# An explicit sequence of all operations in place of a list scheduler

## The chip, the cores and the metric

The kernel runs on one core of a Trainium2 chip. A core has five instruction queues that matter here: TensorE (PE, matrix products; its weight loads are listed as PEld), VectorE (DVE), ScalarE (ACT), GpSimd (POOL) and SyncE (SP, which issues nearly all DMAs). Each queue runs its instructions in the order in which the program holds them; an instruction waits for the semaphores of those it depends on, and what is behind it in the same queue waits with it. The metric is the device time of one execution in microseconds (us).

## The reference

One transformer block on x of 2048 rows by 640 columns, in fp32:

```python
h  = x + A(layernorm(x))                 # wqkv 640 x 1920, wo 640 x 640
h2 = h + B(layernorm(h))                 # w_gate, w_up 640 x 1728, w_down 1728 x 640
# A: 32 heads of 20; row s attends to rows s, s-2, ..., s-14 (rows < 0 masked)
logits = einsum("bhsd,bhswd->bhsw", q, kg) * 20 ** -0.5
o      = einsum("bhsw,bhswd->bhsd", softmax(logits), vg)      # then o @ wo
# B
g = silu(x @ w_gate); u = x @ w_up; return (g * u) @ w_down
```

## The kernel before

**Tiling.** The 2048 rows are worked on in four blocks of 512 rows, each of four tiles of 128. The 640 columns are five chunks of 128 for contraction, and four groups of 160 (eight heads) for attention. The FFN's 1728 columns are 14 slices of 128 (the last is half full). Each fp32 operand of a product is split into a high and a low part of the fp32r type, and each product takes three passes: high by high, low by high, high by low. ScalarE makes the high parts by a cast, VectorE the low ones by a subtraction.

**Stages of a block.** x is loaded and normalised; TensorE transposes it into a PSUM bank (L604), ScalarE and VectorE split it into high and low (L606, L607). The wqkv weights are loaded (L616) and split (L617, L619), and projected with (L643, 480 columns at a time); the results are evicted (L648) and stored to DRAM, from where attention loads q, k and v back in a layout with eight shifted rows. Attention is mostly VectorE's: a product of 128x2560 elements for q times k (L692), a reduction of it (L699), softmax (L706 to L723), the product with v (L727), and a tree of additions (L735). The output is transposed, multiplied by wo (L890), and added to x. Then the second normalisation (L507 writes its low parts into `shb`) and the FFN: for each slice the weights are loaded (L938) and split (casts L939 for gate and up, L940 for down, subtraction L956; low parts are kept in DRAM and loaded again in later blocks, L951 and L944). TensorE computes the gate into bank 5 (in the listings `bank_73`) and the up projection into bank 6 (`bank_74`), 15 matmuls each (L962). ScalarE applies silu to bank 5 (L985), VectorE multiplies by bank 6 (L986), the result is split (L996, L997) and the down products (L973) gather in banks 0 to 4. In the last two blocks some slices are done in pairs, with combined operands that need fewer products (L1046, L1068, L1093, L1103), and the remaining down products come at the very end (L1298), followed by the last additions (L1109).

Attention of one block and the FFN of another run side by side: the VectorE instructions of attention fill the time in which TensorE does the FFN.

**What sets the order.** No engine's program is written out by hand. Each operation (one or several instructions of one engine) is recorded by `P.add(engine, cost, function, reads, writes, priority, ...)`; there are 2846, and their dependencies follow from the addresses that they read and write. At the end `for n in P.order(): P.ops[n][2]()` emits them, so the sequence of `order()` is the order of each queue. Before, `order()` first simulates the five engines and the DMA lanes by the recorded costs and takes the ready operation with the best priority (`listed`), then goes nine times through a round (`ROUNDS`) in which due times are worked out backwards (`latest`) and the simulation is repeated with them. Each operation's place is its simulated start plus, for some 320 operations, a number of us from the table `SHIFT`; the result is the topological order by that key.

## Time and profile before

| | |
|---|---|
| timed runs | median 837.33 us of 3 (836.17 to 838.05) |
| profiled execution | span 835.3 us (it has no time of its own beside the span) |
| granted clock of TensorE | 0.999 |
| TensorE busy | 826.3 us (99%), 4061 matmuls |
| VectorE busy | 755.7 us (90%), 916 instructions |
| ScalarE busy | 421.3 us (50%), 740 instructions |
| GpSimd busy | 23.1 us (3%) |
| DMA | 211.08 MB, mean 253 GB/s |

The span goes from the first to the last instruction of the profiled execution. "Busy" is the time in which an engine had an instruction in work; the idle time between is put down to what ended it. In rows such as `L986 DVE TENSOR_TENSOR fa<-bank,fa ... x34 | 23.2, 682 | 4.1 <-ACT fa L985 2.1` one reads the line, the engine, the operation, its output and inputs, the count, the busy time in us and the mean of one in ns, and after the second bar the engine's idle time just before these instructions with what ended most of it. In a row of waits, `PE bank L604 <- DVE sha L607: 1.4, 1, 1.4`, the first part is the instruction that waited, the second what it waited for, then the total in us, the number of waits and the longest.

### The profile page before, as it was taken

The numbers are of one execution on the slowest core, as the hardware profiler recorded it, in microseconds if no ns is written. First come the engines' busy times: TensorE is split into PE (matmuls) and PEld (weight loads), VectorE is DVE, ScalarE is ACT, GpSimd is POOL, SyncE is SP. The second block draws the span as 40 slices with busy tenths as digits, with TensorE's granted clock in tenths as the row PEclk, the third lists the DMA queues.
The fourth block names the chain that finished last, engine by engine and source line by source line (L and its number), as shares of the span: only waits on it lengthen the run. The fifth ranks groups of instructions, "written<-read, shape, count | busy, mean of one in ns | idle before, by whom it ended". The sixth has DMA issues, their size and how long they took to land.

```text
span 835.3 us, 11299 instructions
## 1 busy us (share of the span) xinstructions
PE 826.3 (99%) x4061; PEld 712.8 (85%) x4061; DVE 755.7 (90%) x916; ACT 421.3 (50%) x740; POOL 23.1 (3%) x34
## 2 busy tenths in 40 slices
PE   8999999999999999999999999999999999999998
PEld 6888888889978888887888888888988888888998
DVE  7599999999999999999999999998869888777982
ACT  7856473333783435654543476565695323323440
POOL 0000000000100000001000000000000000000000
PEclk9999999999999999999999999999999999999999
DMA  8897868568679764899899758899999634457722
GB/s 274 288 348 275 267 213 283 185 207 308 186 219 343 257 197 177 326 303 349 282 313 349 271 173 315 255 288 352 352 339 320 224 115 151 124 175 258 273 99 75
DMA packets 113223, 211.08 MB, mean 253 GB/s; under 512 B 37952, under 2 KB 70400, under 8 KB 112528
## 3 DMA queue, kind: packets, MB, share of 16 engines
q1 hardware_dynamic: 112864, 209.96, 74.0%
q8 instruction: 32, 0.52, 0.2%
q10 hardware_dynamic: 304, 0.41, 0.1%
q14 instruction: 23, 0.19, 0.1%
HBM read 151.27 MB, written 59.05 MB: 252 GB/s over the span
## 4 chain that ended last, share of the span: by engine, by line
PE 84%; DVE 8%; ACT 3%; DMA 3%; issue 1%; SPq 0%; POOL 0%; DVEq 0%; ACTq 0%; POOLq 0%
PE bank L962 22%; PE bank L1046 18%; PE bank L643 15%; PE bank L973 10%; PE bank L1298 7%; PE bank L890 6%; DMA fa<-in_x_dram 2%; PE bank L1103 1%; DVE fa L692 1%; PE bank L1093 1%; DVE fa L735 1%; PE bank L1068 1%; DVE fa L727 1%; DVE fa L699 1%; ACT ra L617 1%
## 5 line engine op out<-in xcount | busy, mean ns | idle before, releaser
L962 PE MATMUL bank<-shb,ra 128*128 128x512 f32 x810 | 190.0, 390 | 1.3 <-DVE shb L507 1.3
L962 PEld LDWEIGHTS bank<-shb,ra 128*128 128x128 f32 x810 | 151.4, 188 | 32.7 <-ACT shb L506 1.5
L643 PE MATMUL bank<-ra,sha 128*128 128x480 f32 x480 | 105.2, 379 | 0.2 <-ACT ra L617 0.2
L643 PE MATMUL bank<-ra,shb 128*128 128x480 f32 x470 | 102.5, 378 | 0.0
L643 PEld LDWEIGHTS bank<-ra,sha 128*128 128x128 f32 x480 | 89.8, 188 | 14.5 <-ACT ra L617 0.6
L643 PEld LDWEIGHTS bank<-ra,shb 128*128 128x128 f32 x470 | 88.1, 188 | 13.2
L692 DVE TENSOR_TENSOR fa<-fa 128x2560 f32<-128x2560 f32 x32 | 90.2, 2820 | 0.9 <-DMA fa<-qsc 0.4
L727 DVE TENSOR_TENSOR fa<-fa 128x2560 f32<-128x2560 f32 x32 | 90.3, 2822 | 0.8
L699 DVE TENSOR_REDUCE fa<-fa 128x128 f32<-128x2560 f32 x32 | 89.9, 2810 | 0.4
L1046 PE MATMUL bank<-shb,ra 128*128 128x512 f32 x360 | 89.4, 395 | 0.6 <-DVE fa L990 0.6
L973 PE MATMUL bank<-ra,acts 128*128 128x512 f32 x328 | 80.7, 391 | 0.0
L1046 PEld LDWEIGHTS bank<-shb,ra 128*128 128x128 f32 x360 | 66.0, 188 | 16.2 <-DVE fa L1223 1.7
L735 DVE TENSOR_TENSOR fa<-fa 128x1280 f32<-128x1280 f32 (+2 forms) x70 | 76.7, 1096 | 1.3
L890 PE MATMUL bank<-ra 128*128 128x320 f32 x480 | 74.1, 310 | 0.0
L890 PEld LDWEIGHTS bank<-ra 128*128 128x128 f32 x480 | 71.7, 188 | 2.4 <-ACT fa L893 1.0
L648 ACT ACTIVATE st<-bank,fa 128x480 f32<-128x480 f32 x64 | 41.0, 656 | 64.1 <-PE bank L643 59.5
L973 PEld LDWEIGHTS bank<-ra,acts 128*128 128x128 f32 x328 | 61.1, 188 | 13.2 <-DVE acts L997 0.5
L1046 PE MATMUL bank<-ra 128*128 128x512 f32 x288 | 69.1, 390 | 0.0
L1046 PEld LDWEIGHTS bank<-ra 128*128 128x128 f32 x288 | 53.9, 188 | 11.1
L1223 DVE TENSOR_TENSOR fa<-bank,fa 128x512 f32<-128x512 f32 x60 | 41.0, 689 | 19.8 <-PE bank L1046 19.0
L939 ACT CAST ra<-fa 128x1280 fp32r<-128x1280 f32 (+1 forms) x38 | 45.6, 1207 | 22.9 <-PE bank L962 12.3
L996 ACT CAST acts<-fa 128x512 fp32r<-128x512 f32 x34 | 21.0, 620 | 48.7 <-DVE fa L986 47.0
(189 smaller groups left out, 1059.8 us busy)
## 6 DMA issues: line engine op xcount, KB each, us to landing
fa<-in_ffn_dram SPq DMA_DIRECT2D x28, 960.0 KB, 6.4
fa<-ksc SPq DMA_DIRECT2D x16, 880.0 KB, 5.4
fa<-vsc SPq DMA_DIRECT2D x16, 880.0 KB, 7.3
ra<-lsc SPq DMA_DIRECT2D x21, 640.0 KB, 5.8
ra<-lsc SPq DMA_DIRECT2D x27, 320.0 KB, 3.7
lsc<-ra SPq DMA_DIRECT2D x13, 640.0 KB, 4.6
fa<-in_ffn_dram SPq DMA_DIRECT2D x12, 640.0 KB, 4.0
ra<-tsc SPq DMA_DIRECT2D x8, 960.0 KB, 7.1
```

Source lines behind the costliest of these rows:

```text
L643: T.matmul(banks[bk][:, 0:480], l, r_(wq(g, w, c), 480), start=(p, c) == first_mm, stop=(p, c) == last_mm)
L648: P.add("ACT", act(480) + 0.06, lambda bk=bk, j=j: A.activation(stage_t()[:, so : so + 1920].rearrange("p (t j c) -> p t j c", t=3, j=NJ)[ ...
L692: P.add("DVE", dve(2560), lambda: V.tensor_tensor(f(PROD, 2560).rearrange("p (j w c) -> p j w c", j=2, w=W), window(ko, 2 * jp), f(qo + 32 ...
L699: P.add("DVE", dve(2560), lambda: V.tensor_reduce(f(lo + 128 * jp, 128), f(PROD, 2560).rearrange("p (n d) -> p n d", d=DH), axis=AX.X, op= ...
L727: V.tensor_tensor(f(PROD, 2560).rearrange("p (j w d) -> p j w d", j=2, d=DH), bass.AP(tensor=fa[:, vo : vo + 160].tensor, offset=fa[:, vo ...
L735: V.tensor_add(dst(v), v[:, :, 0:m, :], v[:, :, m : 2 * m, :])
L890: T.matmul(banks[bk][:, 0:320], l, r_(m, 320), start=p == 0 and c == 0, stop=p == 2 and c == NC - 1)
L939: P.add("ACT", act(n), lambda: A.copy(r_(gu, n), f(raw, n)), r=[rf(raw, n)], w=[rr(gu, n)], prio=PR["fh"])
L962: T.matmul(banks[bk], r_(gu + 1280 * w + wid * c + col, 128), x2(a, c), start=p == 0 and c == 0, stop=p == 2 and c == NC - 1)
L973: T.matmul(banks[bk][:, lo:hi], l, m, start=first and p == 0, stop=last and p == len(passes) - 1)
L1046: T.matmul(banks[bk], r_(ws[w] + 256 * q, 128), x(a, c), start=start and p == n == q == 0, stop=stop and p == 2 and n == len(terms) - 1 an ...
L1298: T.matmul(banks[bks[j]][:, 0:320], t(a, 128, 128 * j), r_(ws[w], 320), start=p == q == 0, stop=p == NP - 1 and q == 2)
```

## The change

The table `SHIFT`, the rounds, `listed` and `latest` are removed. `ORDER` is a tuple of all 2846 operation numbers; `order()` is now the topological order by the place in it. The operations, their numbers, their dependencies and their tiles are the same: 4061 matmuls, 916 VectorE instructions and 586 DMAs of SyncE in both programs; only ScalarE has 33 loads of an activation table where it had 32, as its functions come in another succession. Since the file has another length, a line of the part after the table has a number higher by 12 (L962 becomes L974, L985 becomes L997, L986 becomes L998), and three tiles have other numbers behind their names.

```diff
-LANES, HOP = 8, 0.035
-LAP = {"PE": 0.0, "ACT": 0.1, "DVE": 0.08, "POOL": 0.0, "SP": 0.0}
...
-SHIFT = {
-    7: 3.5, 9: -106.8, 22: 0.4, 31: -515.8, 32: -221.5, 33: -238.8, 34: -84.5, 35: -34.6, 36: -483.8, 37:
...
+ORDER = (
+    0, 6, 11, 42, 3, 10, 7, 9, 2, 31, 32, 34, 12, 13, 15, 8, 16, 17, 39, 33, 36, 37, 118, 43, 22, 14, 40, 119, 38,
...
     def order(self):
-        start = self.listed()
-        for stretch, serial, dma in ROUNDS:
-            start = self.listed(self.latest(start, stretch, dma), serial)
-        self.start, self.end = start, max(t + o[1] for t, o in zip(start, self.ops))
-        ops = self.ops
-        left = [len(o[3]) for o in ops]
-        key = [(t + SHIFT.get(n, 0.0), n) for n, t in enumerate(start)]
-        heap, out = [key[n] for n in range(len(ops)) if not left[n]], []
+        left = [len(o[3]) for o in self.ops]
+        succ = [[] for _ in self.ops]
+        for n, o in enumerate(self.ops):
+            for d in o[3]:
+                succ[d].append(n)
+        place = {n: i for i, n in enumerate(ORDER)}
+        heap, out = [(place.get(n, n), n) for n in range(len(left)) if not left[n]], []
         heapq.heapify(heap)
         while heap:
             n = heapq.heappop(heap)[1]
             out.append(n)
-            for m in self.succ[n]:
+            for m in succ[n]:
                 left[m] -= 1
                 if not left[m]:
-                    heapq.heappush(heap, key[m])
+                    heapq.heappush(heap, (place.get(m, m), m))
         return out
```

The moves are spread over the whole program: on TensorE 808 operations lie on average 4.0 places from where they were (at most 65), on ScalarE 579 by 3.3, on VectorE 855 by 4.3 (at most 92), on SyncE 586 by 6.1 (at most 103); GpSimd is unchanged. Three places follow, each as rows of one engine's queue: line, operation, output and inputs, size, and how many in a row.

**The start on TensorE**, before: matmuls that warm the array up (L554, `bank_72`), transposes of x (L604) and the first QKV projections (L643).

```order
L554 MATMUL bank_72<-ra 128x512 x10
L604 MATMUL bank_75<-fa 128x128
L604 MATMUL bank_74<-fa 128x128 x8
L554 MATMUL bank_72<-ra 128x512
L604 MATMUL bank_73<-fa 128x128 x3
L604 MATMUL bank_75<-fa 128x128 x4
L643 MATMUL bank_69<-ra,sha_128 128x480
L604 MATMUL bank_74<-fa 128x128 x4
```

and now:

```order
L566 MATMUL bank_72<-ra 128x512 x11
L616 MATMUL bank_74<-fa 128x128 x4
L616 MATMUL bank_75<-fa 128x128
L655 MATMUL bank_68<-ra,sha_124 128x480 x2
L655 MATMUL bank_68<-ra,sha_125 128x480
L655 MATMUL bank_68<-ra,sha_124 128x480 x2
L616 MATMUL bank_74<-fa 128x128 x4
```

Five transposes instead of sixteen stand ahead of the first projection, and further tiles' transposes come between projections. On SyncE the first loads were one of x with 64 rows, three tiles of x, then eight of wqkv; now they are that of 64 rows, one wqkv, one tile of x, six wqkv, two tiles of x. On ScalarE two casts of wqkv now stand ahead of the first cast of the transposed x.

**The gates near 450 us on TensorE**, around one slice's up projection into `bank_74`; `bank_73` is the gate's, and rows with `acts` are down products. Before:

```order
L962 MATMUL bank_74<-shb,ra 128x512 x15
L973 MATMUL bank_72<-acts,ra 128x512 x3
L973 MATMUL bank_68<-ra,acts 128x512 x3
L973 MATMUL bank_69<-ra,acts 128x512 x3
L973 MATMUL bank_70<-ra,acts 128x512 x3
L973 MATMUL bank_71<-ra,acts 128x512 x3
L962 MATMUL bank_73<-shb,ra 128x512 x15
L962 MATMUL bank_74<-shb,ra 128x512 x15
```

and now (the first row of `bank_74` ends the same slice's projection, the second begins the next slice's):

```order
L985 MATMUL bank_72<-acts,ra 128x512 x9
L985 MATMUL bank_68<-ra,acts 128x512 x3
L974 MATMUL bank_74<-shb,ra 128x512 x5
L985 MATMUL bank_69<-ra,acts 128x512 x6
L985 MATMUL bank_68<-ra,acts 128x512 x3
L974 MATMUL bank_74<-shb,ra 128x512 x5
L985 MATMUL bank_70<-ra,acts 128x512 x3
```

Projections come in pieces of five between down products, and the next slice's up projection begins ahead of its gate projection: `bank_74` is written again after nine matmuls, where thirty lay between before (three in each of five groups, and fifteen of the gate).

**VectorE near 500 us**, around the multiply that reads `bank_74` (L986, now L998), among instructions of attention. Before:

```order
L723 TENSOR_TENSOR fa<-fa 128x256
L896 TENSOR_TENSOR h_1559<-h_1559,fa 128x640
L727 TENSOR_TENSOR fa<-fa 128x2560
L735 TENSOR_TENSOR fa<-fa 128x2x640
L986 TENSOR_TENSOR fa<-bank_74,fa 128x512
L735 TENSOR_TENSOR fa<-fa 128x2x2x160
L727 TENSOR_TENSOR fa<-fa 128x2560
```

and now:

```order
L735 TENSOR_TENSOR fa<-fa 128x256
L739 TENSOR_TENSOR fa<-fa 128x2560
L747 TENSOR_TENSOR fa<-fa 128x2x640
L747 TENSOR_TENSOR fa<-fa 128x2x2x160
L739 TENSOR_TENSOR fa<-fa 128x2560
L747 TENSOR_TENSOR fa<-fa 128x2x640
L998 TENSOR_TENSOR fa<-bank_74,fa 128x512
```

Three attention instructions that stood behind the multiply now stand ahead of it.

93 lines of the change are left out of this document (1 added, 92 removed), and 175 rows, old and new, of tables (ORDER, SHIFT).

## The prediction

> **What bounds the kernel now.** I read the page's totals first, then the forty slices, then the shares of the chain of waits.
>
> ```profile
> PE 826.3 (99%) x4061; PEld 712.8 (85%) x4061; DVE 755.7 (90%) x916; ACT 421.3 (50%) x740; POOL 23.1 (3%) x34
> PE   8999999999999999999999999999999999999998
> PE 84%; DVE 8%; ACT 3%; DMA 3%; issue 1%; SPq 0%; POOL 0%; DVEq 0%; ACTq 0%; POOLq 0%
> ```
>
> TensorE is busy for 826.3 of 835.3 us, and only the first and the last slice show a gap; the chain that ended last runs through it for 84%. The reordering changes no operation, so the only thing to gain is idle time of TensorE, 9.0 us in all. The view by windows tells where that lies (from:to, the window's length, then busy time and count of PE, PEld, DVE, ACT and POOL, the granted clock, the DMA share and GB/s):
>
> ```profile
> 0.00:20.00 20.00, 16.99 (x73) 13.81 (x74) 15.96 (x46) 15.39 (x40) 1.16 (x7) 1.00 0.84 273
> 180.00:240.00 60.00, 58.62 (x315) 52.91 (x314) 59.36 (x58) 33.71 (x72) 3.90 (x4) 1.00 0.69 224
> 400.00:460.00 60.00, 60.00 (x266) 49.51 (x265) 59.45 (x57) 26.24 (x35) 1.72 (x2) 1.00 0.94 322
> 770.00:835.30 65.30, 61.45 (x419) 61.19 (x418) 46.64 (x83) 21.62 (x36) 0.00 (x0) 0.99 0.45 159
> ```
>
> 3.0 us are idle in the first 20 us, 1.4 between 180 and 240, and 3.85 in the last window. The last cannot move: the final matmuls end at 769.86 + 60.29 = 830.15 us (chain row below), and the last additions and the stores of the output follow. The waits of TensorE name the rest:
>
> ```profile
> PE bank L604 <- DVE sha L607: 1.4, 1, 1.4
> PE bank L554 <- POOL ra L1401: 1.3, 1, 1.3
> PE bank L962 <- DVE shb L507: 1.3, 1, 1.3
> PE bank L1046 <- DVE fa L990: 0.6, 1, 0.6
> PE bank L604 <- DVE fa L443: 0.2, 1, 0.2
> PE bank L643 <- ACT ra L617: 0.2, 1, 0.2
> ```
>
> The L554 row is the start of the program (nothing can be ahead of it). The five others add up to 3.7 us. **That is the most that an order can win among waits shown as idle**; a loss has no such limit, because VectorE is 59.45 of 60 us busy in the window 400 to 460 and has nothing to give back when TensorE is kept waiting for it.
>
> **The head.** From the timeline of the start:
>
> ```profile
> 1.31 4.64 PE L554 MATMUL bank<-ra 128*128 128x512 f32 x10 [1.31 <-POOL ra L1401]
> 3.31 4.69 SPq L616 DMA_DIRECT2D fa<-in_wqkv_dram  x8
> 8.41 0.66 PE L604 MATMUL bank<-fa 128*128 128x128 f32 x4 [1.40 <-DVE sha L607]
> 11.22 11.09 PE L643 MATMUL bank<-ra,sha 128*128 128x480 f32 x50
> ```
>
> Before, sixteen transposes L604 stand ahead of the first QKV projection L643, and at 8.41 four of them wait 1.40 us for L607 to empty their bank; the projections run without a break from 11.22. In the new order five transposes stand ahead of it, so that wait can go (at most −1.4). Against it, SyncE now puts one wqkv load ahead of all but the first x load and six more ahead of the last two, and ScalarE has two wqkv casts ahead of its cast of the transposed x. A wqkv cast takes 0.599 us (the L617 row below), so if both were in the way the projections would start 1.2 us later. I take −0.4, between −1.4 and +1.2 and on the side of the gain, since eleven transposes fewer stand ahead of the projections, but the row at 3.31 puts 4.69 us on the issuing of the eight loads, which the casts now need sooner. A second spot is the last wqkv load:
>
> ```profile
> 50.15 0.59 ACT L617 CAST ra<-fa 128x480 fp32r<-128x480 f32 x1 [1.17 <-DMA fa<-in_wqkv_dram]
> 50.79 3.54 PE L643 MATMUL bank<-ra,sha 128*128 128x480 f32 x14 [0.16 <-ACT ra L617]
> L617 ACT CAST ra<-fa 128x480 fp32r<-128x480 f32 x20 | 10.9, 599 | 1.2 <-DMA fa<-in_wqkv_dram 1.2
> ```
>
> Its cast waited 1.17 us for the data, and TensorE stood for it. That load moves from SyncE's 43rd to its 28th transfer, so the wait goes: −0.2 from the row, up to −0.6 with the weight load that was held with it; I take −0.4.
>
> **The gates.** This is the largest term. For each FFN slice of 128 columns, 15 matmuls L962 fill bank 5 (gate), 15 fill bank 6 (up); ScalarE reads bank 5 (silu, L985), VectorE reads bank 6 (multiply, L986). The next L962 into the same bank must wait for that reader, and everything else of TensorE is queued behind it. So what counts is the matmul work that TensorE has between a bank's last L962 and its next write: the cover. I add it up from the order of the matmuls by their measured pace, from the chain of waits (start, us, line, count):
>
> ```profile
> 267.17 6.80 PE bank L962 x30
> 769.86 60.29 PE bank L1298 x411
> ```
>
> 6.80 / 30 = 0.227 us for a 512-column matmul, 60.29 / 411 = 0.147 us for a 320-column one. At the multiply near 450 us, the old order has five groups of three down matmuls and 15 projections into the other bank behind it: 15 x 0.227 + 15 x 0.227 = 6.8 us. The new order writes bank 6 again after nine matmuls: 9 x 0.227 = 2.04 us. Over all 34 gates the median cover of bank 6 falls from 6.8 to 4.2 us, and the gates with 3.5 us or less go from 8 to 12; for bank 5 the median falls from 6.8 to 3.6, and they go from 11 to 16. What must fit under it at that place is in the timeline:
>
> ```profile
> 444.32 6.96 PE L962 MATMUL bank<-shb,ra 128*128 128x512 f32 x30
> 450.18 2.82 DVE L699 TENSOR_REDUCE fa<-fa 128x128 f32<-128x2560 f32 x1
> 452.91 0.68 DVE L986 TENSOR_TENSOR fa<-bank,fa 128x512 f32<-128x512 f32 x1
> 454.52 1.75 PE L962 MATMUL bank<-shb,ra 128*128 128x512 f32 x7
> ```
>
> The projections end at 451.28. VectorE is inside a 2.82 us attention reduction until 452.9, so the bank is free at 453.59: 2.31 us after its last matmul. With 6.8 us of cover that costs nothing; with 2.04 us the same delay would cost 0.27. In the worst case the 2.82 us instruction starts just as the projections end: 2.82 + 0.68 − 2.04 = 1.5 us. The groups show that short cover is not by itself a stall:
>
> ```profile
> L986 DVE TENSOR_TENSOR fa<-bank,fa 128x512 f32<-128x512 f32 x34 | 23.2, 682 | 4.1 <-ACT fa L985 2.1 <-PE bank L1046 1.2 <-PE bank L962 0.8
> L985 ACT ACTIVATE fa<-bank 128x512 f32<-128x512 f32 x34 | 20.3, 598 | 39.8 <-PE bank L962 30.2 <-DMA asc<-fa 6.3 <-PE bank L1068 1.6
> L692 DVE TENSOR_TENSOR fa<-fa 128x2560 f32<-128x2560 f32 x32 | 90.2, 2820 | 0.9 <-DMA fa<-qsc 0.4
> PEld bank L962 <- ACT fa L985: 0.2, 1, 0.2
> ```
>
> Before, the 19 places with short cover cost only 0.2 us in one place, since each had been given a reader that comes early (the silu is mostly early enough to wait 30.2 us for TensorE). The new order has nine more such places. At the price of before they cost nothing (9 x 0.2 / 19 = 0.1), at the worst price 13.5 us. The new order puts fewer multiplies straight behind a 2.8 us instruction (5 where it was 15), which speaks for the low end; but at one place near 500 us it puts three attention instructions more ahead of the multiply and leaves it 4.5 us where it had 6.8. I take 0.2 us for each, near the 0.27 of the example: **+1.8**.
>
> **Weight casts ahead of a silu.** In the new order nine silus stand directly behind the 1.2 us cast of the gate and up weights (L939), where it was two; those behind the short cast L940 fall from 17 to nine.
>
> ```profile
> L939 ACT CAST ra<-fa 128x1280 fp32r<-128x1280 f32 (+1 forms) x38 | 45.6, 1207 | 22.9 <-PE bank L962 12.3 <-DMA fa<-in_ffn_dram 8.8 <-PE bank L1068 1.7
> ACT ra L939 <- DMA fa<-in_ffn_dram: 8.8, 3, 4.9
> SPq L938 <- DVE ra L956: 20.6, 8, 7.5
> ```
>
> L939 waited for its load three times of 38, 2.9 us in the mean and 4.9 at the longest; the SyncE row shows why a load can be late: its issue stands behind VectorE. A silu behind a waiting cast waits too, then its multiply, then TensorE. The cast and the silu (1.21 + 0.60) fit under the 3.6 us of median cover with 1.8 to spare, so a mean wait would cost 2.9 − 1.8 = 1.1 and the longest 3.1. Seven more casts by 3/38 is about half a wait: 0.6 to 1.7; I take **+1.2**, with nothing at the low end, and 8.8 if all that was measured came onto TensorE. SyncE's queue is the most reshuffled (some issues move by a hundred places), so the share of late loads may itself change, in either direction.
>
> **A table load.** The new program has 33 loads of an activation table where the old had 32.
>
> ```profile
> 495.23 1.28 ACT L985 ACT_TABLE_LOAD   x1
> 496.52 0.60 ACT L985 ACTIVATE fa<-bank 128x512 f32<-128x512 f32 x1
> ```
>
> It takes 1.28 us on ScalarE, which is busy for half of the span; its idle time hides it: 0, or 1.28 if a silu stood right behind it with no cover left. The Trainium skill (ScalarE: Activation LUTs, What ACT_TABLE_LOAD costs) puts a switch at 1283 ns of load and about 1380 ns of drain, 2.66 us together. The trace agrees on the load, but shows no drain here: the silu starts 0.01 us after it. By the page's figure the upper end of this term would be 2.66, and the sum the same.
>
> **The sum.** −0.4 − 0.4 + 1.8 + 1.2 + 0 = +2.2 us, on a span of 835.3: 837.5. The profiled execution has no time of its own beside its span; the timed runs have a median of 837.33, 2.0 above that span. So the forecast is 837.33 + 2.2 = **839.5 us**. A measurement can tell about 0.2% from no change, 1.7 us: faster means under 835.7, slower over 839.0.
>
> **The forecast and its rivals.** (a) Moderately slower, as summed: 839.0 to 843. 0.37.
>
> (b) The new order takes away waits and adds none: the readers of the banks come early everywhere, and 1.4 at L604, 1.3 at L962, 0.6 at L1046 and 0.4 go. All of it gives 837.33 − 3.7 = 833.6; two thirds of it 834.9. It decides once the waits that go outweigh those that come by 1.7 us, so the new ones must stay under 2.0. For it speaks the fall from 15 to 5 of multiplies behind a long instruction, which frees bank 6 sooner than the cover alone tells; against it that it needs nearly all of the listed waits, of which the L962 one hangs on a LayerNorm chain (L507) that no listing shows shortened. 0.26.
>
> (c) No change: the head gains about 0.8 and the gates cost as much, 837.3. For it speaks that 19 short covers cost 0.2 us so far. 0.24.
>
> (d) Loads become late: SyncE is one queue, its weight loads L938 stand behind stores that wait for VectorE (7.5 us at the longest), and two of the nine casts L939 before a silu wait 4.9 us as the longest did. Each costs 3.1 beyond the cover: +6.2 on the head's −0.8 and the gates' +1.8, 844.5. It decides from the point where a load lands over 1.8 us after its cast is next on ScalarE; two more such would give 850.7. 0.13.
>
> **How the numbers follow.** (a) and (d) are slower: 0.50; (b) faster: 0.26; (c) 0.24. The predicted time is the sum, 839.5; the likeliest case alone reaches from 838.5 to 843. The range that leaves out the lowest third of (b) and the far half of (d) goes from 834.3 to 846.
>
> **What would show it.** The head: the row of L604 behind L607 is gone or below 1 us, and projections start before 11.2. The last wqkv load: no L617 wait of TensorE near 50 us. The gates: in the waits of TensorE or its weight loads, rows L974 behind L998 or L997 (the new line numbers of L962, L986, L985), five or more of them, 1 to 4 us together, near 450 and 500 us. The casts: ScalarE's wait of L951 for in_ffn_dram in four or more places, followed by a late silu. Wrong would be the whole picture if TensorE's idle time falls below 7.5 us (then b), or if its busy time rises by more than 1 us with the same 4061 matmuls (then matmuls are stretched by something other than these waits), or if new waits lie mainly behind 580 us, where cover hardly changed.

## The result

The explicit sequence takes **852.48 us** in the median (851.43 to 852.86, 4 runs) against 836.99 for the old order: a ratio of 1.0183 [1.0168, 1.0197], 15.5 us slower. The prediction said 839.5 and at most 846: right that it gets slower, but by seven times the 2.2 us of the sum, and far outside the range.

The totals of the page of the profile after, and its shares of the chain of waits:

```profile
PE 833.6 (98%) x4061; PEld 716.3 (84%) x4061; DVE 758.7 (89%) x916; ACT 419.3 (49%) x741; POOL 24.2 (3%) x34
...
PEclk9999999999989999999999999999999999999999
...
PE 42%; DVE 37%; DMA 9%; ACT 6%; issue 4%; SPq 2%; POOL 0%; DVEq 0%; ACTq 0%; POOLq 0%
```

The work is the same, but TensorE's busy time has grown by 7.3 us with the same 4061 matmuls, one of the forty slices has a lower clock, and the chain that ended last no longer runs through TensorE alone: VectorE has 37% of it where it had 8. Where the time went is in the view by windows, first one row of before that the prediction did not need:

```profile
240.00:320.00 80.00, 80.00 (x374) 67.34 (x373) 79.64 (x87) 33.31 (x48) 1.82 (x3) 1.00 0.79 271
```

and then three of after (length, busy time and count of PE, PEld, DVE, ACT, POOL, granted clock, DMA share, GB/s):

```profile
240.00:320.00 80.00, 76.56 (x321) 62.57 (x321) 73.26 (x80) 33.21 (x46) 2.27 (x3) 0.94 0.79 265
...
400.00:460.00 60.00, 59.97 (x265) 49.22 (x263) 59.26 (x59) 25.39 (x33) 2.45 (x3) 1.00 0.85 294
460.00:540.00 80.00, 78.55 (x385) 66.50 (x384) 78.02 (x74) 42.75 (x75) 4.67 (x4) 1.00 0.81 279
```

Between 240 and 320 us TensorE gets through 321 matmuls (of several sizes) instead of 374, and **both** engines idle: TensorE 3.4 us, VectorE 6.7 (before 0.0 and 0.4). DMA moved about as much. So there neither engine is the bound; they wait for each other and for transfers.

A measure that takes waits and the lower clock together is the excess: from the trace's timeline, the distance from each matmul's start to the next one's, less the median distance for its size (227 ns for 512 columns, 217 for 480, 147 for 320, 109 for 128). Over the program it is 10.9 us before and 26.2 after; the difference, 15.3, is that of the spans (850.7 less 835.3) to within 0.1. By place, before and after in us: 0 to 20: 5.1, 6.9. 40 to 60: 0.6, −0.1. 220 to 260: 1.8, 6.3. 280 to 300: 0.0, 4.0. 380 to 400: 0.6, 1.7. 440 to 560: 0.4, 4.0. The rest: 2.4, 3.4. The waits of TensorE that are over half a microsecond:

```profile
PE bank L974 <- DVE fa L998: 3.3, 3, 2.1
PE bank L974 <- ACT fa L997: 2.1, 2, 1.4
PE bank L516 <- ACT fa L489: 2.1, 2, 1.4
PE bank L655 <- ACT sha L618: 1.6, 1, 1.6
PE bank L566 <- POOL ra L1413: 1.3, 1, 1.3
PE bank L974 <- ACT shb L518: 0.7, 1, 0.7
PE bank L616 <- DVE sha L619: 0.7, 1, 0.7
PE bank L1058 <- DVE fa L1002: 0.6, 1, 0.6
```

The first two are the forecast's gates and casts (3.3 and 2.1, 5.4 us together). L516 and the L974 behind L518 (2.8) belong to the second normalisation, which the forecast had not priced. Three places in the timeline after show how the waits come about. The normalisation near 240 us (start, length, engine, line, shapes, and in brackets the idle time before and what ended it), before:

```profile
226.05 0.82 DVE L901 TENSOR_TENSOR h<-fa 128x640 f32<-128x640 f32 x1
...
226.78 2.81 DVE L699 TENSOR_REDUCE fa<-fa 128x128 f32<-128x2560 f32 x1
...
229.51 0.81 DVE L901 TENSOR_TENSOR h<-fa 128x640 f32<-128x640 f32 x1
```

and after:

```profile
229.40 2.82 DVE L711 TENSOR_REDUCE fa<-fa 128x128 f32<-128x2560 f32 x1
...
232.13 0.81 DVE L913 TENSOR_TENSOR h<-fa 128x640 f32<-128x640 f32 x1
...
234.00 0.81 DVE L913 TENSOR_TENSOR h<-fa 128x640 f32<-128x640 f32 x1
...
239.61 0.44 PE L516 MATMUL bank<-fa 128*128 128x128 f32 x2 [1.39 <-ACT fa L489]
...
240.75 1.86 PE L516 MATMUL bank<-fa 128*128 128x128 f32 x8 [0.70 <-ACT fa L489]
```

In the old order one of the last two residual additions stands ahead of the reduction of 2.8 us; in the new order both stand behind it. The second starts at 234.00 us where it started at 229.51, 4.5 us later, while TensorE was 1.3 us later just before (its output projection L902 starts at 219.54 us, L890 before at 218.28). What follows the additions (statistics, scaling, transposes, split) is late with them. A multiply near 290 us:

```profile
287.30 0.83 DVE L968 TENSOR_TENSOR ra<-fa,ra 128x640 fp32r<-128x640 f32 x1 [1.86 <-DMA lsc<-ra]
...
291.19 0.69 DVE L998 TENSOR_TENSOR fa<-bank,fa 128x512 f32<-128x512 f32 x1
...
291.94 2.37 PE L974 MATMUL bank<-shb,ra 128*128 128x512 f32 x5 [2.07 <-DVE fa L998]
```

VectorE waits 1.86 us in front of a weight split L968, because the store of the previous low parts has not landed; the multiply stands behind that and TensorE, with 2.04 us of cover in the order, waits 2.07. And a silu near 380 us:

```profile
377.60 1.27 ACT L951 CAST ra<-fa 128x1280 fp32r<-128x1280 f32 x1 [3.58 <-DMA fa<-in_ffn_dram]
378.88 1.28 ACT L997 ACT_TABLE_LOAD   x1
380.17 0.60 ACT L997 ACTIVATE fa<-bank 128x512 f32<-128x512 f32 x1
380.82 1.43 PE L974 MATMUL bank<-shb,ra 128*128 128x512 f32 x5 [1.44 <-ACT fa L997]
```

A weight cast waits 3.58 us for its load, with the silu and its table load behind it. This is the case that the prediction described.

### The profile page after: what moved, and what is told of

The parts are those of the page before. It is cut to its first block, busy times and chain, and to the rows that moved or that the text cites. A ratio compares the mean times of both kernels' runs of the same rounds, so it can differ in the third digit from the quotient of the medians.

```text
span 850.7 us, 11148 instructions
## 1 busy us (share of the span) xinstructions
PE 833.6 (98%) x4061; PEld 716.3 (84%) x4061; DVE 758.7 (89%) x916; ACT 419.3 (49%) x741; POOL 24.2 (3%) x34
## 4 chain that ended last, share of the span: by engine, by line
PE 42%; DVE 37%; DMA 9%; ACT 6%; issue 4%; SPq 2%; POOL 0%; DVEq 0%; ACTq 0%; POOLq 0%
PE bank L1058 16%; PE bank L974 8%; PE bank L1310 7%; DVE fa L704 7%; DVE fa L739 6%; DVE fa L711 6%; DVE fa L747 4%; PE bank L902 3%; PE bank L985 3%; DMA lsc<-ra 2%; PE bank L1115 1%; PE bank L1080 1%; DVE acts L1009 1%; PE bank L1105 1%; DVE fa L524 1%
## 5 line engine op out<-in xcount | busy, mean ns | idle before, releaser
L974 PE MATMUL bank<-shb,ra 128*128 128x512 f32 x810 | 198.9, 395 | 6.2 <-DVE fa L998 3.3
L974 PEld LDWEIGHTS bank<-shb,ra 128*128 128x128 f32 x810 | 153.3, 191 | 40.4 <-DVE fa L998 4.8
L655 PE MATMUL bank<-ra,sha 128*128 128x480 f32 x480 | 107.3, 382 | 1.6 <-ACT sha L618 1.6
L655 PEld LDWEIGHTS bank<-ra,shb 128*128 128x128 f32 x470 | 88.0, 188 | 13.5 <-ACT st L660 0.3
L739 DVE TENSOR_TENSOR fa<-fa 128x2560 f32<-128x2560 f32 x32 | 90.3, 2823 | 0.8
L1058 PE MATMUL bank<-shb,ra 128*128 128x512 f32 x360 | 89.7, 393 | 1.0 <-DVE fa L1002 0.6
L985 PE MATMUL bank<-ra,acts 128*128 128x512 f32 x328 | 86.4, 393 | 0.2 <-DVE acts L1009 0.2
L1058 PEld LDWEIGHTS bank<-shb,ra 128*128 128x128 f32 x360 | 66.3, 188 | 15.7 <-DVE fa L1002 1.0
L902 PE MATMUL bank<-ra 128*128 128x320 f32 x480 | 74.1, 309 | 0.0
L902 PEld LDWEIGHTS bank<-ra 128*128 128x128 f32 x480 | 71.8, 188 | 2.1 <-ACT fa L905 0.7
L985 PEld LDWEIGHTS bank<-ra,acts 128*128 128x128 f32 x328 | 61.5, 189 | 13.8 <-DVE acts L1009 1.0
L660 ACT ACTIVATE st<-bank,fa 128x480 f32<-128x480 f32 x64 | 40.6, 659 | 46.1 <-PE bank L655 34.9
L951 ACT CAST ra<-fa 128x1280 fp32r<-128x1280 f32 (+1 forms) x38 | 45.8, 1205 | 27.0 <-DMA fa<-in_ffn_dram 22.4
L1217 ACT CAST ra<-fa 128x512 fp32r<-128x512 f32 x30 | 18.0, 619 | 46.8 <-PE bank L1058 23.0
```

What stands on the lines that cost most here:

```text
L655: T.matmul(banks[bk][:, 0:480], l, r_(wq(g, w, c), 480), start=(p, c) == first_mm, stop=(p, c) == last_mm)
L660: P.add("ACT", act(480) + 0.06, lambda bk=bk, j=j: A.activation(stage_t()[:, so : so + 1920].rearrange("p (t j c) -> p t j c", t=3, j=NJ)[ ...
L739: V.tensor_tensor(f(PROD, 2560).rearrange("p (j w d) -> p j w d", j=2, d=DH), bass.AP(tensor=fa[:, vo : vo + 160].tensor, offset=fa[:, vo ...
L902: T.matmul(banks[bk][:, 0:320], l, r_(m, 320), start=p == 0 and c == 0, stop=p == 2 and c == NC - 1)
L951: P.add("ACT", act(n), lambda: A.copy(r_(gu, n), f(raw, n)), r=[rf(raw, n)], w=[rr(gu, n)], prio=PR["fh"])
L974: T.matmul(banks[bk], r_(gu + 1280 * w + wid * c + col, 128), x2(a, c), start=p == 0 and c == 0, stop=p == 2 and c == NC - 1)
```

## The experiments

All are timed beside the kernel before; gains are told as the difference of the ratios to it, times 837 us. In the diffs a row is one engine's instruction as in the order listings; "old" and "new" are the two sequences of operation numbers.

### One late reader at a time

Theory A said that the loss is a sum of separate waits, each curable where it stands; theory B that VectorE is as full as TensorE and hands a wait on. Four kernels change the new sequence at one kind of place each.

The multiply at 291 us (VectorE):

```diff
+L998 TENSOR_TENSOR fa<-bank_74,fa 128x512
 L968 TENSOR_TENSOR ra<-fa,ra 128x640
 L734 RECIPROCAL fa<-fa 128x32
 L968 TENSOR_TENSOR ra<-fa,ra 128x640
 L1009 TENSOR_TENSOR acts<-fa,acts 128x512
 L735 TENSOR_TENSOR fa<-fa 128x256
-L998 TENSOR_TENSOR fa<-bank_74,fa 128x512
```

> The explicit sequence with one move on VectorE: the multiply L998 that ended TensorE's 2.07 us wait at 291.9 us goes ahead of two splits L968, the quotient L734, L1009 and L735, right behind L733. Nothing else moves. Theory A (the loss is a sum of separate waits of TensorE, each caused by one instruction that stands too far back, and each long one is followed by some us at half clock): the wait of 2.07 us goes, and the eight matmuls at half clock behind it (1.6 us) with it: 852.5 - 3.7 = 848.8 us. Theory B (VectorE is as full as TensorE from 60 to 580 us, so a wait taken from TensorE comes back at the next late reader): 851.5 to 852.5 us, with a new or longer wait of L974 within the next 60 us.

Measured: 850.95 us, ratio 1.0174 [1.0153, 1.0194], 0.8 us less than the new sequence, not told apart from it. In its trace the excess from 280 to 300 us is 0.1 (4.0 before the move), but from 300 to 320 it is 2.8 (0.0). The wait was cured, and most of it came back one slice later: theory B. (The excess from 80 to 100 us is 1.6 where it was 0.1; that is ahead of the move and cannot come from it.)

The normalisation near 230 us (VectorE):

```diff
+L913 TENSOR_TENSOR h_1639<-fa 128x640 x2
 L711 TENSOR_REDUCE fa<-fa 128x128
-L913 TENSOR_TENSOR h_1639<-fa 128x640
 L777 STREAM_TRANSPOSE fa<-fa 128x2x5x32
 L968 TENSOR_TENSOR ra<-fa,ra 128x640
-L913 TENSOR_TENSOR h_1639<-fa 128x640
+L469 ... L472
 L704 TENSOR_TENSOR fa<-fa 128x2560
...
-L469 ... L472
```

> The explicit sequence with three moves on VectorE near 230 us: the two additions L913 of the second block-0 tile pair go ahead of the 2.8 us reduction L711 that stood before them at 229.4, and the four small LayerNorm instructions L469 to L472 go ahead of the 2.8 us multiply L704 that follows. Nothing else moves. Theory A: the normalisation reaches TensorE's transposes L516 about 2.8 us earlier, so the waits of 1.39, 0.70 and 0.68 us at 239.6, 240.8 and 243.3 go and the eleven matmuls at half clock behind them (2.2 us) too; minus 4 to 5: 848 us. Theory B: the attention work is now later by what was moved ahead of it, and the span falls by under 1 us: 851.5 to 852.5.

Measured: 855.11 us (849.46 to 856.84), ratio 1.0207 [1.0168, 1.0245]: no gain. The timeline of this kernel, first near 245 us:

```profile
242.92 2.81 DVE L711 TENSOR_REDUCE fa<-fa 128x128 f32<-128x2560 f32 x1
...
246.88 5.46 PE L974 MATMUL bank<-shb,ra 128*128 128x512 f32 x17 [3.78 <-DVE shb L519]
```

The waits for L489 are gone, and a longer one for L519 is there: the reduction that had stood ahead of the additions now stands ahead of the split L519. Another row of the same timeline is a wait at another place, which no move here touches:

```profile
93.19 3.11 PE L655 MATMUL bank<-ra,shb 128*128 128x480 f32 x7 [3.49 <-ACT st L660]
```

It is missing from the profile of the new sequence, and 1.3 to 3.5 us long in those of six kernels that keep its first hundred microseconds; ScalarE's eviction L660 waits there for a store of v to free its buffer. So the time at this place differs from run to run of one order, and what it costs is not lost twice. In the profiles with an excess of 0.1 to 1.6 us from 80 to 100 us, that from 220 to 260 is 6.3 to 6.7; in those with 4.0 to 7.0 it is 1.7 to 2.9 (all kernels with the new order at both places, this one aside). Both places together have 6.1 to 8.7 us, and 1.7 before. VectorE is busy for 176.7 of the 180 us from 60 to 240, so a TensorE that was held up at 93 us has less to wait for at 240.

The casts at 378 and 540 us (ScalarE):

```diff
-L951 CAST ra<-fa 128x1280
 L997 ACT_TABLE_LOAD
 L997 ACTIVATE fa<-bank_73 128x512
+L951 CAST ra<-fa 128x1280
```

> The explicit sequence with two moves on ScalarE: the 1.27 us weight cast L951 at 377.6 us (which waited 3.58 us for its load) and the one at 539.9 us go behind the silu L997 that followed each. Nothing else moves. Theory A: TensorE's waits of 1.44 us at 380.8 and 0.70 us at 543.1 for L997 go: 852.5 - 2.1 = 850.4 us. Theory B: 852 to 852.5, as the next late reader takes the wait over.

Measured: 850.52 us, ratio 1.0163 [1.0148, 1.0178]: 1.7 us less, close to theory A's 2.1, though its interval still touches that of the new sequence. The excess from 380 to 400 us falls from 1.7 to 0.4; the excess near 543 us stays at 1.1, as TensorE now waits there 0.7 us for the moved cast itself.

The start:

```diff
-ORDER = new
+ORDER = old[:142] + [n for n in new if n not in old[:142]]
```

> The first 142 operations in the order of before (up to TensorE's 73rd matmul, some 20 us), the rest in the order of the explicit sequence. Theory A: TensorE loses 1.75 us more in the first 20 us of the explicit sequence than in the old one (1.60 us of waiting for ScalarE's L618 behind a cast that waits for wqkv, and 0.66 us for L619), and gets it back: 850.7 us. Theory B (the start does not matter, since VectorE's attention sets the pace from 60 us on and starts when the loads allow): 852 to 853.

Measured: 852.26 us, ratio 1.0182 [1.0158, 1.0205]: no gain. Its first 20 us have 6.9 us of excess with the old start, as the new one had. In the profiles of the kernels with the old start that number goes from 4.6 to 6.9, with the new from 5.3 to 6.9: no effect of the start is to be seen. What goes with most of the difference is the clock: the first 20 us have a granted clock of 0.91 in the new sequence and in this kernel, and 1.00 before, and both kinds occur with either start.

### SyncE's queue alone

In the waits of SyncE the row of attention's output stores had grown and was now the largest (before, then after):

```profile
SPq L769 <- DVE fa L765: 20.9, 10, 6.0
```

```profile
SPq L781 <- DVE fa L777: 74.2, 20, 10.7
```

These stores wait for VectorE's transposes. Theory C: they hold back loads and stores that are ready. Against it stands that all waits of SyncE together are 534 us before and 537 after (the largest before was L678 behind VectorE's L692, 47.0): for the most part another instruction had come to stand at the head of the queue. The first test puts every DMA in the order in which the trace says that it became ready, in the new sequence and, as a control, in the old:

```diff
-SyncE's operations in the order of the sequence
+SyncE's operations sorted by the end of the last operation that each depends on (from the trace)
```

> The explicit sequence with only SyncE's queue changed: its 586 DMAs stand in the order in which, by the trace of the explicit sequence, what each waits for was done, so that none that is ready stands behind one that is not; an issue moves by 4.5 places on average. The other four queues are those of the explicit sequence. Theory C (SyncE's queue is the cause: it stood 74.2 us waiting for VectorE's L777 ahead of the stores L781, where it was 20.9, and held back the stores and loads behind them, for which VectorE and ScalarE then waited): 840 to 845 us, VectorE's idle time between 240 and 320 us under 2 us (6.7 before this edit), the wait of L781 under 40 us. Theory B (TensorE and VectorE wait for each other because the banks have too little cover, whatever SyncE does): 850 to 853.

> The old sequence with only SyncE's queue changed in the same way (the order in which, by the trace of the old sequence, what each DMA waits for was done; 1.4 places on average). Theory C: SyncE's order hardly costs anything here, as its stores waited 20.9 us and no engine idled for them: 835 to 837.5. Theory B: 836 to 838 too; a result above 839 would say that the order of readiness is itself a bad one, and that a gain of the same edit in the explicit sequence is to be put down to its waits alone.

Measured: 867.56 us (1.0369 [1.0354, 1.0385]) in the new sequence, 15.6 us **more**; and 843.48 us (1.0085 [1.0067, 1.0102]) in the old, 7.1 us more by moves of 1.4 places on average. SyncE's wait for L777 did fall, but VectorE idled 10.9 us between 240 and 320 us, where theory C had said under 2. From the waits of the new sequence so sorted:

```profile
SPq L781 <- DVE fa L777: 32.9, 13, 8.8
...
PE bank L516 <- ACT fa L489: 4.7, 2, 4.0
PE bank L655 <- ACT st L660: 4.1, 1, 4.1
PE bank L1058 <- DMA ra<-lsc: 3.6, 1, 3.6
```

TensorE now waits at other places, once 3.6 us for a load itself. Theory C fell in this form. What the pair shows is that SyncE's order is worth 7 to 16 us even when nothing else moves, and that ready first is a bad rule for it.

So the queue was exchanged between the two kernels:

```diff
-SyncE in the kernel's own order
+SyncE in the other kernel's order, as far as dependencies allow
```

> TensorE, ScalarE, VectorE and GpSimd in the explicit sequence, word for word; SyncE's DMAs in the old order as far as the dependencies allow (on average 1.2 places from the old order, 5.6 from the new). Theory C, after two runs in which a small change of SyncE's order alone cost 7 and 15 us (the order in which loads and stores are issued decides most of the loss): 838 to 845 us. Theory B (the loss comes from the order of the computing engines, that is from short cover of the banks and from what stands ahead of the readers): 850 to 853 us. Anything between gives the share of each.

> The reverse: TensorE, ScalarE, VectorE and GpSimd in the old order, word for word; SyncE's DMAs in the new order as far as the dependencies allow (0.9 places from the new, 5.7 from the old). Theory C: 845 to 852 us. Theory B: 836 to 839 us. If the two shares add up, this run and the one before it lie together as far above the old kernel as the explicit sequence does (some 16 us).

Measured: 923.21 us (1.1025 [1.1001, 1.1049]) with the new computing engines and the old SyncE, 945.03 us (1.1294 [1.1267, 1.1322]) the other way round. Both theories fall: neither part is at fault by itself, since each with the other's partner is five to seven times as bad as the new sequence. One row of waits from the first kernel and one from the second:

```profile
PE bank L655 <- ACT st L660: 23.6, 3, 13.3
```

```profile
SPq L694 <- DVE fa L739: 49.3, 7, 20.3
```

In a queue that waits in order, a transfer that stands too early stops all behind it: one wait of SyncE for VectorE's L739 is 20.3 us long. The longest wait in the first row, 13.3 us, is for an eviction that stands on ScalarE behind a cast, L540, which itself waits 21.64 us for its load. A share of the loss cannot be read from such an exchange.

### By stretches of the program

Here all queues change together at a cut, where both sequences hold the same operations but for a few.

```diff
-ORDER = new
+ORDER = new to 205 us, then old to 330 us, then new
```

> The explicit sequence up to its 205th microsecond, then the operations that the old sequence has up to its 330th, in the old order on all queues, then the rest of the explicit sequence. Theory A (the loss sits where the trace shows it, 8.7 us of the 15 between 205 and 330): 843 to 845 us. Theory B or C as causes that act all along the program: a gain of under 4 us, 848.5 to 852, since the late loads and the waits of VectorE behind 330 us stay.

Measured: 848.39 us in 2 runs (1.0139 [1.0115, 1.0164]), 3.7 us less, at the edge of what B and C allow and short of A. From 240 to 320 us the excess is 1.1 (8.7 in the new sequence), but 5.2 at the seam from 220 to 240, where TensorE waits 1.62 us for ScalarE's cast L891 and 1.60 for VectorE's split L892. A cut inside a stretch has a price of its own, so the program was split once, near 322 us, where the two sequences differ by 19 operations:

```diff
-ORDER = new
+ORDER = old to 322 us, then new        # first kernel
+ORDER = new to 331 us, then old        # second kernel
```

> The old order on all queues up to the 322nd microsecond (the two sequences hold the same operations there but for 19), the explicit sequence behind it. Counting the time by which TensorE's matmuls are apart by more than their pace, the explicit sequence loses 16.3 us up to 320 us and 9.9 behind, the old one 6.9 and 4.0. Theory A (losses add up by place): 837 + 5.9 = 843 us. Theory E (what the explicit sequence loses behind 320 us is what it brought along as lateness from before, of VectorE above all): 837 to 839. Theory B in its strong form (VectorE's attention sets the pace to 580 us and TensorE's waits are only its echo): the same as E.

> The reverse: the explicit sequence up to its 331st microsecond, the old order behind it. Theory A: 837 + 9.4 = 846.4 us. Theory E: as the explicit sequence, 851 to 853. The two runs together are as far above the old kernel as the explicit sequence if losses add up by place.

Measured: 842.63 us (1.0057 [1.0042, 1.0072]) with the old first part, 848.70 us (1.0127 [1.0110, 1.0145]) with the old second part. 0.57% and 1.27% are 1.84%, and the new sequence has 1.83%. **The loss of the two parts adds up**: about 5 us come from behind 322 us and 10.6 from ahead of it, against 5.9 and 9.4 as counted from the trace. The intervals leave about 2 us of room in this sum. Theory E (lateness carried along) falls, as it had said 837 to 839 for the first kernel. Within a part, though, the waits are tied to one another: ahead of the cut, the second kernel has 4.0 us of excess from 80 to 100 us and 2.2 from 220 to 260, where the new sequence has 0.1 and 6.3.

### Several repairs together

The two moves on casts, the multiply at 291 us, and two more multiplies:

```diff
+L998 TENSOR_TENSOR fa<-bank_74,fa 128x512
 L722 TENSOR_REDUCE fa<-fa 128x32
 L723 TENSOR_TENSOR fa<-fa 128x256
-L998 TENSOR_TENSOR fa<-bank_74,fa 128x512
...
+L998 TENSOR_TENSOR fa<-bank_74,fa 128x512
 L739 TENSOR_TENSOR fa<-fa 128x2560
 L747 TENSOR_TENSOR fa<-fa 128x2x640
-L998 TENSOR_TENSOR fa<-bank_74,fa 128x512
```

> The explicit sequence with the moves of the first and the third run (the multiply at 291 us, the casts at 378 and 540 us) and two more on VectorE: the multiply at 465.8 us goes ahead of L722 and L723, the one at 516.1 us ahead of L739 and L747. Theory A: 852.5 - 1.5 - 2.0 (as measured one by one) - 0.52 - 0.76 (the waits of TensorE that those two ended) = 847.7 us. Theory B: 850 to 852, since what is taken from one wait is lost at the next.

Measured: 852.27 us, ratio 1.0169 [1.0148, 1.0189]: 1.2 us less and not told apart from no gain, where the parts promised 4.8 (3.8 with the gains of the first and the third run as told here, 0.8 and 1.7). The cured places are cured (380 to 400: 0.2; 460 to 480: 0.0; 500 to 520: 0.0), and others behind them have taken over (300 to 320: 3.7; 520 to 540: 2.1): from 280 to 560 us the excess is 8.2, and 9.7 in the new sequence. Repairs of single readers do not add up.

### The price of a late reader, and the half clock

Near 243 and 292 us the new sequence has matmuls at half pace behind a wait. Windows of its trace: a stretch with the first waits near 240 us and the one behind it, the same for the wait at 292 us, and one behind the 1.44 us wait at 380.8 us:

```profile
237.50:240.92 3.42, 1.33 (x8) 0.67 (x7) 3.25 (x8) 3.35 (x9) 0.00 (x0) 1.00 0.56 207
240.92:247.75 6.83, 6.16 (x19) 4.83 (x19) 6.80 (x14) 6.74 (x12) 0.00 (x0) 0.50 1.01 348
288.70:292.12 3.42, 1.35 (x7) 0.81 (x6) 3.42 (x7) 0.29 (x2) 0.00 (x0) 1.00 0.64 167
292.12:295.53 3.41, 3.41 (x9) 2.64 (x10) 3.38 (x2) 0.41 (x1) 0.00 (x0) 0.50 1.02 336
380.80:384.80 4.00, 3.98 (x17) 3.30 (x18) 3.79 (x3) 0.00 (x0) 0.00 (x0) 1.00 0.57 182
```

To measure this alone, one multiply of the **old** kernel is made late:

```diff
+                def mul(late=6 if len(P.ops) == 1317 else 0):      # 10 in the second kernel
+                    for _ in range(late):
+                        V.tensor_copy(f(so, 512), f(so, 512))
+                    V.tensor_mul(f(so, 512), banks[6], f(so, 512))
```

> The old kernel with one multiply made late: ahead of the multiply L986 that starts at 363.4 us and whose bank has 1.13 us of cover, VectorE copies its operand onto itself six times (nothing of the result changes). It measures the price of one late reader and of the half clock by itself. Theory A: TensorE waits 2 to 3.5 us there, the next 8 to 10 matmuls run at 0.43 us instead of 0.23 (1.6 to 2 us), and the whole is later by both, 4 to 5 us. Theory D (the half clock has another cause than the wait): the wait alone, 2 to 3.5 us, with the clock at 1.00.

> The old kernel with the multiply near 363 us made later still: ten copies ahead of it where the run before had six (2.73 us of copies, a wait of 1.56 us, the span 2.0 us longer, the clock at 1.00). Theory A: the wait is 3.4 us, and now the matmuls behind it run at half clock for some 3 to 4 us as they did behind the wait of 2.07 us in the explicit sequence (1.6 to 2 us more): the span 5 to 5.5 us over the old one. Theory D (waits of this size leave the clock alone, the half clock at 243 and 292 us had another cause): 3.4 to 3.9 us, the clock at 1.00.

Measured, one run each: 839.45 us beside 836.29 and 841.58 beside 837.65, so 3.2 and 3.9 more; the spans are 837.3 and 839.4, 2.0 and 4.1 over that of the old profile. One run of each leaves about 1 us open. The row of the wait in the timeline and the row of the windows behind it, for six copies and then for ten:

```profile
365.88 4.87 PE L962 MATMUL bank<-shb,ra 128*128 128x512 f32 x20 [1.56 <-DVE fa L990]
```

```profile
365.00:372.00 7.00, 6.12 (x27) 5.04 (x28) 6.90 (x8) 3.52 (x5) 0.00 (x0) 1.00 0.68 179
```

```profile
366.80 6.15 PE L962 MATMUL bank<-shb,ra 128*128 128x512 f32 x20 [3.39 <-DVE fa L990]
```

```profile
365.00:372.00 7.00, 5.20 (x17) 4.20 (x18) 6.83 (x9) 2.30 (x3) 0.00 (x0) 0.76 0.41 112
```

Behind 1.56 us the clock stays, behind 3.39 us it drops, and the excess there is 5.0: the wait and 1.6, nearly all of it at half pace. So a wait does bring the half clock, as theory A said, if it is long enough (theory D was right for the first kernel); the last section shows what is long enough. Its price for the whole is less certain: the span grew by 4.1, not 5.0, and the four timed runs of the new sequence have mean clocks from 0.992 to 0.998 with spans of 850.7 and 850.4 at the two ends.

### Five stores

In the old order the stores of attention's output stand behind the stores that were ready before them; in the new order five transfers do not:

```diff
-L781 DMA osc<-fa 32x5x64 x2
 L694 DMA fa<-vsc 128x1x1760
 L666 DMA vsc<-st 64x2x640
+L781 DMA osc<-fa 32x5x64 x2
...
-L781 DMA osc<-fa 32x5x64
-L950 DMA fa<-in_ffn_dram 128x1920
 L963 DMA lsc<-ra 128x640
 L963 DMA lsc<-ra 128x1280
-L781 DMA osc<-fa 32x5x64
 L963 DMA lsc<-ra 128x640
+L950 DMA fa<-in_ffn_dram 128x1920
+L781 DMA osc<-fa 32x5x64 x2
```

> The explicit sequence with five DMAs moved on SyncE by two to five places and nothing else: two stores of attention's output (L781) that wait for VectorE's transposes at 84.5 and 87.8 us go behind the store L666 of v that was ready at 79.9; and the two L781 and the weight load L950 that wait for VectorE at 276 to 278 us go behind the three stores L963 of low parts that were ready at 247, 255 and 271. In the old order these L781 stand behind those stores. Theory C, locally (a store that is ready stands behind one that waits for VectorE; its buffer stays taken, and ScalarE's L660 at 92 us or VectorE's L968 at 287 us waits for it, then TensorE): the 1.9 us wait of VectorE at 287 and TensorE's 2.07 us at 292 with the half clock behind it go, and so does TensorE's varying wait at 93 us (0 to 3.5): 846 to 849 us. Theory B: 851 to 852.5.

> The same five moves on SyncE and the two on ScalarE of the third run (each gave 2.0 us there). Theory C with sums by place: 2 us under the run before, 844 to 847 us. Theory B: as the third run alone, 850 to 851.

Measured: 850.19 us (1.0146 [1.0118, 1.0174]), 3.1 us less than the new sequence, though its interval still touches that; with the two casts 848.53 us (1.0134 [1.0114, 1.0155]), 4.1 us less, the first repair that is clear of it, and 2.4 less than with the casts alone. Both times lie between what the theories had said. Two rows of the new sequence's timeline:

```profile
80.53 0.53 SPq L666 DMA_DIRECT2D vsc<-st  x1
...
89.48 1.21 ACT L660 ACTIVATE st<-bank,fa 128x480 f32<-128x480 f32 x2 [0.23 <-DMA vsc<-st]
```

and rows of that of the first of these kernels:

```profile
83.33 0.53 SPq L666 DMA_DIRECT2D vsc<-st  x1
...
92.71 1.21 ACT L660 ACTIVATE st<-bank,fa 128x480 f32<-128x480 f32 x2 [0.23 <-DMA vsc<-st]
...
93.98 2.37 PE L655 MATMUL bank<-ra,shb 128*128 128x480 f32 x5 [4.18 <-ACT st L660]
...
288.34 0.82 DVE L968 TENSOR_TENSOR ra<-fa,ra 128x640 fp32r<-128x640 f32 x1 [1.30 <-ACT ra L951]
...
292.97 1.43 PE L974 MATMUL bank<-shb,ra 128*128 128x512 f32 x5 [1.59 <-DVE fa L998]
```

The store of v that was moved is issued earlier (85.22 us; 88.77 in the new sequence), but it is not the one that the eviction waits for. By the semaphores of both traces that is the store of v before it, issued at 83.33 us (80.53 in the new sequence), which lands 9.3 us later (8.8); so this move could not cure the wait at 93 us. Near 288 us VectorE no longer waits for the store but for the cast L951, whose load is late, and TensorE waits 1.59 us instead of 2.07, with the clock at full pace. That this is the work of the moves is not shown: in the kernels where only the start or only the casts were changed, TensorE waits 1.41 and 1.36 us at this place, at full pace too. So the moves of the five transfers save about 2 to 3 us, measured with and without the casts and each time to within some 2 us, and the traces do not show where; theory C holds for a part of the loss at most.

No version beat the old order.

## Why the prediction was wrong

**The step that failed** is the sum. It took 3.0 us for the gates and casts, whose waits alone came to 5.4; it had no term for the second normalisation, where the excess rose by 4.5 us in the profile; and it had none for the half clock, 4.9 us by the matmuls' distances, which lies within these stretches and the head. The direction was right, and so was the mechanism of the gates and casts.

**The bound**: right, and understated. TensorE is the bound of the old order and can win at most 3.7 us; that VectorE "has nothing to give back" decided more than any single term. Where both are near full, a repair on one engine pushes something else behind (the normalisation run, the repairs together).

**The head, −0.4**: not told from nothing. The wait of L604 for L607 fell from 1.4 to 0.7 and one of 1.6 for L618 came, since ScalarE's second wqkv cast ahead of it waited for its load; but with the old start put back the excess was the same. **The last wqkv load, −0.4**: the wait went as said; the excess from 40 to 60 us fell by 0.7.

**The gates, +1.8, and the casts, +1.2**: the right mechanism at the named places, mis-sized. The forecast said five or more waits behind L998 or L997, 1 to 4 us together; there are five, of 5.4. The multiply whose cover falls to 2.04 us near 450 cost 0.52 (0.27 in the example), the one near 500 us 0.76, one at 292 us with the same cover 2.07, the casts ahead of a silu at 380 and 543 us 1.44 and 0.70, and L951 waited for its load nine times instead of three (22.4 us for 8.8). The row from which the low end came, 0.2 us for 19 short covers, was the price in an order in which each short cover had an early reader; it says nothing of one in which they do not. The term was within its own bounds (13.5 and 8.8), but the range was not drawn from them.

**The normalisation**: left at nothing without a reason. Rival (b) named the wait of L962 behind L507 and said that no listing shows its chain shortened. It was not asked whether it was lengthened, and it was: the excess from 220 to 260 us rose by 4.5 us, the largest single place in this profile. That both additions L913 stand behind a reduction of 2.8 us is plain in VectorE's order. That their place is the cause is argued, not shown: with the additions moved ahead of it, the wait came back at the split behind them. In runs with a long wait at 93 us less is lost here.

**The half clock** was in no term. It takes 2.5 us of TensorE's time from 240.9 to 247.7 us (nine matmuls of 512 columns at 0.427 instead of 0.227, seven of 128 at 0.213 instead of 0.109), 1.6 near 292 us (eight of 512), and 0.8 near 10 us. This is most of the 7.3 us by which TensorE's busy time grew. The prediction had named a growth of more than 1 us as the sign that matmuls are stretched by something other than the waits that it counted; the sign came.

**The table load, 0**: right as to the extra one, which stands in a statistic. But loads of a kind that was there before now stand between a late cast and a silu (378.9 us), 1.28 us more on the path.

**Rival (d)**, loads late by SyncE's queue, at 0.13, was nearest in its number, 844.5 (850.7 with two more late casts). Its place was wrong in part: besides L951's loads, stores that keep a buffer taken (L963 ahead of VectorE's split, L666 ahead of ScalarE's eviction) stand ahead of waits. Its price counted two late casts, while excess came at some eight places over 500 us. The reordering of SyncE by six places on average was called a risk in either direction and given no price of its own; the runs show that moves of 1.4 places alone can cost 7 us.

**Still open**: which moves make up the 10.6 us ahead of the cut and how they divide between SyncE's order and VectorE's, since each is fitted to the other and an exchange breaks both; where the moves of the five stores gain; and why the store of v that the eviction at 93 us waits for is issued at 80.5 us in one run and up to 83.6 in others (it lands 8.1 to 9.3 us behind its issue in all of them).

## What to carry to other kernels

Where two engines and the DMA queue are all near full, an order is one fitted whole: price a reordering by place, engine by engine and for every chain that crosses engines (normalisations and stores as well as the visible waits). A wait that the old trace lacks is no sign that its new price is small. A queue that waits in order deserves the first look: compare, for each producer that it waits for, whether anything ready has come to stand behind it.

## What the runs showed of the hardware

The clock falls behind shorter waits than expected, and the clock records of the 18 traces show what counts. Behind the first matmuls, which run at half pace, the granted clock is 1.0 or 0.5, and while matmuls run it changes only at points that lie a whole number of 3.41 us apart; half clock lasts 3.41 us or two to four times that. In the new sequence it is 8.81 to 12.22, 240.92 to 247.75 and 292.12 to 295.53 us. Take each stretch of 3.41 us between two such points, at full clock, and count in it the time by which matmuls stand apart beyond their pace. All 45 stretches with 2.1 us or more of it were followed by half clock, none of the 38 with 1.4 to 2.0, and four of the eight between. The wait of 2.07 us at 292 us lies in one such stretch, and those of 1.39 and 0.70 near 240 us lie in one together. The 1.56 us that six copies made are divided between two (0.94 and 0.89), and the clock stayed. So a wait of about 2 us can cost nothing more or 1.6 us more, as it happens to lie. In the first 20 us the stretch in question has 1.74 us of it before, where the clock stayed, and 2.04 after, where it fell; with the old start and six copies later on it has 2.39, and the clock fell too.

The Trainium skill (TensorE: Matmul & The Clock Gate, Part 1: The HAM clock gate) puts the fall after at least one idle window of about 3.4 us. The traces agree on the half pace (0.427 us for 512 columns) and on the length of 3.41 us, but here a window that was idle for 2.1 us of it was enough.

That moving SyncE's DMAs by 1.4 places on average costs 7.1 us, and by some six places 70 to 110, with every other queue unchanged, was not expected either. The Trainium skill (DMA: Bandwidth & Descriptors, Anatomy of one DMA — SWDGE (gpsimd) path) says that any semaphore wait of a DMA happens on the issuing sequencer before dispatch; the rows of SyncE's waits agree, with single waits of 10.7 us in the new sequence and 20.3 us in the exchange, during which SyncE issued nothing.
